# Loading granule 5's keys and queries ahead of granule 4's values, and releasing the loads of granules 6 and 7 at another point

## The chip, the cores and the metric

The kernel runs on one core of a Trainium2 chip. The metric is device microseconds of one execution; lower is better. Engines are named as in the profile: PE is TensorE's matmuls, PEld its weight loads, DVE is VectorE, ACT is ScalarE, POOL is GpSimd, SP is SyncE.

## The reference

Attention of 4 batches x 8 heads x 768 rows x 64, with a mask (8 global keys, 96 local ones) and a linear bias, followed by a two-layer feed-forward block with a squared ReLU:

```python
scores = scale * np.matmul(q, k.transpose(0, 1, 3, 2))
scores = np.where(keep, scores + bias, -1000000000.0)
a = softmax(scores)                     # (cut)
x = np.matmul(a, v)                     # -> (3072, 512)
h = x @ w_in                            # 512 -> 2048
out = (s * np.maximum(h, 0)**2 + b) @ w_out
```

## The kernel before

The 3072 rows are cut into 12 granules of 256 (numbered 0 to 11, three in each batch; all numbers here count from 0). For each granule GpSimd loads keys, queries and values (128 KB each piece, cast from f32 to bf16), the keys and queries are transposed (by TensorE for granules 0 to 3, by DMA transposes from SyncE from granule 4 on), then TensorE makes scores and weighted sums, and the sums, transposed once more (tile xT, below "transposed sums"), go into the feed-forward block. Work of several granules is interleaved by hand so that TensorE always has something to do.

```python
    def load_granule(j):                      # k and q of both blocks, then v
        ...
        load_v(j)

    def hold_loads(ap):                       # a 1x1 copy on GpSimd: later loads wait for `ap`
        g = work.tile([P, 1], BF16, name="gate", tag="gate")
        nc.gpsimd.tensor_copy(g[0:1, :], ap)
    # (cut)
    def qk_by_dma(j):                         # four DMA transposes of one granule
        for i in range(GB):
            for n in range(2):
                nc.sync.dma_start_transpose(qk_of(b, n)[:, g * GB + i], nat[j][:, n, i, :, :]...)
    # (cut)
    def finish_granule(j):
        if j < X_PE:
            x_by_pe(j)                        # transposed sums by TensorE
        else:
            x_by_dma(j)                       # transposed sums by DMA
        if 6 <= j + LEAD < NJ:                # LEAD = 4
            hold_loads(xT[j][0:1, 0, GT - 1 : GT])
            load_granule(j + LEAD)
    # (cut: the order in which granules 3 to 5 are loaded)
    for i in range(GB):
        load_qk(4, i)
    load_v(3)
    load_v(4)
    load_granule(5)
```

The softmax here doesn't subtract the row's maximum and nothing guards it: scores larger than these inputs give would overflow.

Of the kernel before, what the change touches and what calls it, by code (L numbers as in the profile page):

```python
# [17 lines left out]
def kernel(  # L18
# [19 lines left out]
    DM = H * D  # L38
    DF = moe_w_in.shape[1]
    GB = 2  # L40
# [5 lines left out]
    NJ = B * NGR  # L46
# [22 lines left out]
    LEAD = 4  # L69
# [12 lines left out]
    def nat_tile(j):  # L82
        if j not in nat:
            nat[j] = ldp.tile([P, 2, GB, H, D], BF16, name="nat", tag=f"nat{j % 4}", bufs=1)
        return nat[j]
# [3 lines left out]
    def rows_of(src, b, sb):  # L89
        return src[b, :, sb * P : (sb + 1) * P, :].rearrange("h p d -> p h d")  # L90
# [8 lines left out]
    def load_qk(j, i):  # L99
        b, g = divmod(j, NGR)  # L100
        for n in range(2):
            nc.gpsimd.dma_start(nat_tile(j)[:, n, i, :, :], rows_of(srcs[n], b, g * GB + i))  # L102

    def load_v(j, blocks=range(GB)):
        b, g = divmod(j, NGR)
        for i in blocks:
            sb = g * GB + i
            nc.gpsimd.dma_start(vbuf[b % 2][:, sb, :, 0:D], rows_of(v, b, sb))  # L108

    def load_granule(j):  # L110
        b, g = divmod(j, NGR)
        t = nat_tile(j)
        for i in range(GB):
            sb = g * GB + i
            for n in range(2):
                nc.gpsimd.dma_start(t[:, n, i, :, :], rows_of(srcs[n], b, sb))  # L116
        load_v(j)


    def hold_loads(ap):  # L120
        g = work.tile([P, 1], BF16, name="gate", tag="gate")
        nc.gpsimd.tensor_copy(g[0:1, :], ap)  # L122
# [119 lines left out]
    def template(hs):  # L242
        for h in hs:
            nc.scalar.activation(tmpl[:, h, 0:3, :], late_bf[:, 0:3, :], ACT.Exp, scale=slopes[h])
# [25 lines left out]
    xn = {}  # L270
# [312 lines left out]
    def x_by_pe(j, evac=(nc.vector.tensor_copy, nc.scalar.copy)):  # L583
        t = xT_tile(j)
        nk = KC // len(evac)
        for e, ev in enumerate(evac):
            ps = ps_h.tile([P, nk, GT], BF16, name="ps_x", tag="psh")
            for kc in range(nk):
                for i in range(GB):
                    c = (e * nk + kc) * P  # L590
                    nc.tensor.transpose(
                        ps[:, kc, i * P : (i + 1) * P], xn[j][:, i, c : c + P], ident_bf[:]
                    )
            ev(t[:, e * nk : (e + 1) * nk, :], ps[:])  # L594

    def x_by_dma(j):
        t = xT_tile(j)
        for i in range(GB):
            nc.sync.dma_start_transpose(t[:, :, i * P : (i + 1) * P], xn[j][:, i, :])
# [350 lines left out]
    def finish_granule(j):  # L950
        if j < X_PE:
            x_by_pe(j)
        else:
            x_by_dma(j)
        if 6 <= j + LEAD < NJ:
            hold_loads(xT[j][0:1, 0, GT - 1 : GT])
            load_granule(j + LEAD)

    def step(s, c0, c1, c2, pool=None, pre=()):
# [22 lines left out]
        if last:  # L982
            finish_granule(j)
            if SHIFT < j + 2 < NJ:
                load_voff(j + 2)
# [92 lines left out]
    for i in range(GB):  # L1078
        load_qk(4, i)
    load_v(3)  # L1080
    load_v(4)
    load_granule(5)
    template(range(H))
    lo = FC - FC // 4
    p2_mm(0, 0, 0, lo)
# [34 lines left out]
    p2_mm(1, 1, FC // 2 + 3, FC)  # L1120
    p2_hold(1, 1)
    finish_granule(2)
    s6 = scores(6)
    run(s6)
# [12 lines left out]
    make_koff(4)  # L1137
    run(p1[2][6:8])
    finish_granule(3)
    run(scores(8))  # L1140
    make_voff(4)
# [110 lines left out]
```

## Time and profile before

| | before |
|---|---|
| median of 3 runs | 208.91 us (208.49 to 209.06) |
| the profiled run | 209.15 us, span 207.4 us |
| TensorE busy, weight loads busy | 97%, 77% |
| TensorE's one wait for a transfer | 0.51 us, at 69.1 us |

How to read it: in the slices each digit is a fortieth of the span in tenths of busy time. A line of a timeline gives the start, the length, the engine, the source line, the operation and its tiles; idle time and what ended it stand in brackets. The prediction shows the lines.

### The profile page before, as it was taken

The numbers are of one execution on the slowest core, as the hardware profiler recorded it, in microseconds if no ns is written. First come the engines' busy times: TensorE is split into PE (matmuls) and PEld (weight loads), VectorE is DVE, ScalarE is ACT, GpSimd is POOL, SyncE is SP. The second block draws the span as 40 slices with busy tenths as digits, with TensorE's granted clock in tenths as the row PEclk, the third lists the DMA queues.
The fourth block names the chain that finished last, engine by engine and source line by source line (L and its number), as shares of the span: only waits on it lengthen the run. The fifth ranks groups of instructions, "written<-read, shape, count | busy, mean of one in ns | idle before, by whom it ended". The sixth has DMA issues, their size and how long they took to land.

```text
span 207.4 us, 5323 instructions
## 1 busy us (share of the span) xinstructions
PE 202.1 (97%) x2191; PEld 160.1 (77%) x2191; DVE 161.3 (78%) x338; ACT 128.5 (62%) x198; POOL 68.9 (33%) x90
## 2 busy tenths in 40 slices
PE   7999999999999999999999999999999999999993
PEld 2678884557867485878888898888888889888883
DVE  7786599977989856799799974699866696737974
ACT  5875669486976548786664595663695764476200
POOL 8985333799365300810900828200000000000000
PEclk9999999999999999999999999999999999999999
DMA  5999999999999999999999999999570300240006
GB/s 164 172 179 202 207 206 177 155 152 129 110 150 120 151 132 218 155 213 212 152 198 153 125 154 178 194 172 126 52 206 0 95 14 0 56 150 0 0 9 196
DMA packets 110836, 28.17 MB, mean 136 GB/s; under 512 B 97852, under 2 KB 109308, under 8 KB 110812
## 3 DMA queue, kind: packets, MB, share of 16 engines
q0 software_dynamic: 76000, 13.11, 90.1%
q1 hardware_dynamic: 33612, 14.13, 41.7%
q10 hardware_dynamic: 1200, 0.59, 1.1%
q8 instruction: 17, 0.28, 0.6%
q14 instruction: 7, 0.06, 0.1%
HBM read 27.26 MB, written 6.29 MB: 162 GB/s over the span
## 4 chain that ended last, share of the span: by engine, by line
PE 65%; DMA 23%; POOL 9%; issue 1%; DVE 0%; POOLq 0%
PE ps L619 29%; PE ps L819 24%; DMA nat<-in_q_dram 12%; DMA w_in_bf<-in_moe_w_in_dram 6%; PE ps L667 5%; DMA qx<-nat 4%; PE ps_s L441 4%; PE ps_av L495 3%; POOL vb L108 3%; POOL nat L102 3%; POOL w_in_bf L140 2%; POOL nat L116 1%; PE ps_last L819 0%; DVE o_last L828 0%; POOL rel L173 0%
## 5 line engine op out<-in xcount | busy, mean ns | idle before, releaser
L619 PE MATMUL ps<-xT,w_in_bf 128*128 128x256 bf16 x768 | 90.3, 273 | 0.0
L629 ACT ACTIVATE gT<-ps 128x512 bf16<-128x512 f32 x96 | 55.8, 599 | 46.8 <-PE ps L619 46.6
L619 PEld LDWEIGHTS <-w_in_bf 128*128 128x128 bf16 x768 | 73.0, 98 | 9.4 <-DVE xT L594 0.2
L450 ACT ACTIVATE pt<-ps_s 128x1024 bf16<-128x1024 f32 (+1 forms) x44 | 39.3, 946 | 3.3 <-PE ps_s L441 3.3
L667 PE MATMUL ps<-w_out_bf,gT 128*128 128x512 bf16 x128 | 29.7, 380 | 0.0
L457 DVE TENSOR_TENSOR pt<-pt,tmpl 128x1024 bf16<-128x1024 bf16 (+1 forms) x40 | 24.6, 645 | 3.8 <-ACT pt L450 3.7
L819 PEld LDWEIGHTS <-gsum 128*128 128x128 bf16 x256 | 24.1, 98 | 3.7 <-DVE gsum L782 0.5
L108 POOL DMA_DIRECT2D vb<-in_v_dram x24 | 21.4, 906 | 6.9 <-DMA w_out_bf<-in_moe_w_out_dram 3.4
L793 DVE TENSOR_TENSOR gT<-gT 128x1024 bf16<-128x1024 bf16 x20 | 13.7, 686 | 11.7 <-ACT gT L629 11.7
L667 PEld LDWEIGHTS <-gT 128*128 128x128 bf16 x128 | 11.7, 98 | 13.0
L466 DVE TENSOR_TENSOR xn<-ps_av,rc 128x256 bf16<-128x256 f32 x48 | 20.4, 425 | 1.7
L819 PEld LDWEIGHTS <-gT 128*128 128x128 bf16 x200 | 18.6, 98 | 2.3
L465 DVE RECIPROCAL rc<-ps_av 128x4 f32<-128x4 f32 x48 | 8.6, 179 | 12.3 <-PE ps_av L495 10.4
L116 POOL DMA_DIRECT2D nat<-in_k_dram x16 | 14.2, 885 | 9.2 <-DMA nat<-in_k_dram 5.1
L495 PEld LDWEIGHTS <-pt 128*128 128x128 bf16 x320 | 14.4, 97 | 2.7 <-DVE xn L466 0.7
L632 DVE TENSOR_TENSOR gT<-gT 128x512 bf16<-128x512 bf16 x32 | 13.0, 422 | 3.5 <-ACT gT L629 3.3
L495 PE MATMUL ps_av<-vb,pt 128*128 128x65 bf16 x208 | 15.5, 193 | 0.0
L819 PE MATMUL ps<-w_out_bf,gsum 128*128 128x256 bf16 x128 | 15.3, 273 | 0.0
L116 POOL DMA_DIRECT2D nat<-in_q_dram x16 | 14.2, 888 | 2.9 <-DMA w_in_bf<-in_moe_w_in_dram 1.9
L819 PE MATMUL ps<-wsub,gsum 128*128 128x256 bf16 x128 | 15.1, 273 | 0.0
L819 PE MATMUL ps<-w_out_bf,gT 128*128 128x256 bf16 x120 | 13.9, 273 | 0.0
L122 POOL COPY gate<-xT 1x1 bf16<-1x1 bf16 x6 | 1.1, 176 | 35.9 <-DMA xT<-xn 35.9
(112 smaller groups left out, 228.5 us busy)
## 6 DMA issues: line engine op xcount, KB each, us to landing
out_dram<-o_q SPq DMA_DIRECT2D x15, 256.0 KB, 2.6
vb<-in_v_dram POOLq DMA_DIRECT2D x24, 128.0 KB, 8.3
nat<-in_k_dram POOLq DMA_DIRECT2D x22, 128.0 KB, 7.7
nat<-in_q_dram POOLq DMA_DIRECT2D x22, 128.0 KB, 7.6
w_out_bf<-in_moe_w_out_dram POOLq DMA_DIRECT2D x4, 512.0 KB, 16.2
w_in_bf<-in_moe_w_in_dram POOLq DMA_DIRECT2D x4, 256.0 KB, 7.4
w_in_bf<-in_moe_w_in_dram POOLq DMA_DIRECT2D x2, 512.0 KB, 11.3
out_dram<-o_sb SPq DMA_DIRECT2D x4, 256.0 KB, 6.3
```

What stands on the lines that cost most here:

```text
L108: nc.gpsimd.dma_start(vbuf[b % 2][:, sb, :, 0:D], rows_of(v, b, sb))
L116: nc.gpsimd.dma_start(t[:, n, i, :, :], rows_of(srcs[n], b, sb))
L450: nc.scalar.activation(pt[:, :, 0:ncol], ps[:, :, 0:ncol], ACT.Exp, scale=QSCALE)
L457: nc.vector.tensor_tensor(pv, pv, m.rearrange("p h a c -> p h (a c)"), ALU.mult)
L466: nc.vector.tensor_tensor(dst, av[:, :, :, 0:D], rc[:].to_broadcast((P, 2, 2, D)), ALU.mult)
L495: nc.tensor.matmul(av[:, i, hi, 0 : D + 1], lhsT=pt[:, hi, c * P : (c + 1) * P], rhs=vv, start=(n == 0), stop=(n == len(terms) - 1),)
L619: nc.tensor.matmul(ps[:, i, :], lhsT=w_in_bf[:, kc, fc * P : (fc + 1) * P], rhs=xT[j][:, kc, :], start=(kc == 0), stop=(kc == KC - 1),)
L629: nc.scalar.activation(gs, ps[:], ACT.Relu)
L632: nc.vector.tensor_tensor(gs, gs, gs, ALU.mult)
L667: nc.tensor.matmul(po[:], lhsT=g_of(j)[:, fc, tb * P : (tb + 1) * P], rhs=w_out_bf[:, fc, :], start=(fc == 0), stop=(fc == FC - 1),)
L793: outs.append(lambda: nc.vector.tensor_tensor(gs, gs, gs, ALU.mult))
L819: nc.tensor.matmul(ps[:, tb, cs], lhsT=stat[:, fc, tb * P : (tb + 1) * P], rhs=mov[:, fc, cs], start=(fc == 0), stop=(fc == NH - 1),)
```

## The change

Intent: let granule 5's keys and queries land earlier by loading them ahead of granule 4's values, and keep the loads of granules 6 and 7 out of the way of granule 5's transposes by releasing them only at granule 3's last weighted sum. Before, granule 6 was released by granule 2's transposed sums and granule 7 by granule 3's.

```diff
-        if 6 <= j + LEAD < NJ:
+        if j == 3:
+            hold_loads(xn[j][0:1, GB - 1, DM - 1 : DM])
+            load_granule(6)
+            load_granule(7)
+        elif 8 <= j + LEAD < NJ:
             hold_loads(xT[j][0:1, 0, GT - 1 : GT])
             load_granule(j + LEAD)
 (cut)
     load_v(3)
+    for i in range(GB):
+        load_qk(5, i)
     load_v(4)
-    load_granule(5)
+    load_v(5)
```

## The prediction

> **What bounds the kernel now.** I read the page first (busy shares and slices), then the waits of TensorE alone, then the chain that ended last, and then the timelines of TensorE, GpSimd and VectorE around the one wait that mattered. The page:
>
> ```profile
> span 207.4 us, 5323 instructions
> PE 202.1 (97%) x2191; PEld 160.1 (77%) x2191; DVE 161.3 (78%) x338; ACT 128.5 (62%) x198; POOL 68.9 (33%) x90
> PE   7999999999999999999999999999999999999993
> DMA  5999999999999999999999999999570300240006
> ```
>
> TensorE is busy in 38 of 40 slices at nine tenths or more; only the first and last are lower, which are the opening and the tail. All its idle time is 207.4 - 202.1 = 5.3 us. The DMA engines are full for three quarters of the span, so transfers can be late, but that costs time only where TensorE waits. The waits of TensorE's matmuls, complete:
>
> ```profile
> PE ps_w L161 <- DVE idle L151: 1.2, 1, 1.2
> PE ps_s L441 <- DMA qx<-nat: 0.5, 1, 0.5
> ```
>
> The first is the warm-up at the start. The second is the only wait for a transfer in the whole kernel. The chain of waits from 38 to 70 us says where it comes from:
>
> ```profile
> 48.56 11.61 DMA nat<-in_q_dram
> 60.17 0.02 issue
> 60.19 8.86 DMA qx<-nat
> 69.06 0.04 issue
> 69.10 0.57 PE ps_s L441 x14
> ```
>
> A load of queries (granule 5's second block, by its place in the issue order) was issued at 48.56, landed at 60.17, was turned by a DMA transpose from 60.19 to 69.06, and TensorE's scores for granule 5 began again at 69.10. Behind this point the chain is TensorE without a break to 204.1 us, then the last eviction. The timeline of TensorE at that wait, and the same 16 score matmuls eight microseconds later for comparison:
>
> ```profile
> 68.36 0.23 PE L441 MATMUL ps_s<-qx,kx 64*128 64x128 bf16 x2
> 69.10 0.34 PE L441 MATMUL ps_s<-qx,kx 64*128 64x128 bf16 x6 [0.51 <-DMA qx<-nat]
> 69.60 3.63 PE L667 MATMUL ps<-w_out_bf,gT 128*128 128x512 bf16 x16
> ...
> 77.13 0.40 PE L441 MATMUL ps_s<-qx,kx 64*128 64x128 bf16 x8
> 77.37 0.39 PE L441 MATMUL ps_s<-qx,ko 64*128 64x128 bf16 x8
> 77.69 3.63 PE L667 MATMUL ps<-w_out_bf,gT 128*128 128x512 bf16 x16
> ```
>
> Undisturbed, the 16 take 77.69 - 77.13 = 0.56 us until the next group starts; with the wait they take 69.60 - 68.36 = 1.24 us. So the stall delays TensorE's starts by 0.68 us (0.51 is what is left after the modelled tail of the second matmul).
>
> **What the Trainium skill says.** "Perfetto Trace Analysis", section "Identifying the Most-Contended Engine", warns that matmul busy share is no measure of the distance to roofline, and names the weight-load share instead. Here that is 77%, so 97% does not mean peak; but a change in load order removes no matmul, so it can only win idle time, and the section "Optimization Strategy" of that page says to look for the gaps of that engine and the semaphore behind them. The trace has one such gap. "DMA: Bandwidth & Descriptors", section "Issuing engines are not separate DMA queues", says that transfers started by different engines run on the same 16 DMA engines and interleave. The trace agrees: while loads were in flight the transpose of 60.19 took 8.86 us from issue to landing, and one issued at 80.08, in a stretch without new loads, 4.9 us (from the view of the tile qx). The same page, "Queues, rings and completion order", says that on each DMA engine the descriptors of one ring are consumed in ring order, though completion is not strictly first in, first out; the loads of GpSimd from 27 us on landed in issue order, which is what I rest the landing times below on.
>
> **The change part by part.** The built instruction order shows that TensorE, VectorE, ScalarE and SyncE have the same instructions in the same order; only buffer numbers differ. GpSimd has 93 rows instead of 94: one 1x1 gate copy (0.18 us, off the path) falls away. Everything else is the order and release of loads on GpSimd, whose timeline before is:
>
> ```profile
> 49.43 1.77 POOL L108 DMA_DIRECT2D vb<-in_v_dram  x2
> 51.16 0.18 POOL L122 COPY gate<-xT 1x1 bf16<-1x1 bf16 x1
> 51.28 0.88 POOL L116 DMA_DIRECT2D nat<-in_k_dram  x1
> ...
> 56.19 0.88 POOL L116 DMA_DIRECT2D nat<-in_k_dram  x1 [3.05 <-DMA nat<-in_k_dram]
> ...
> 61.62 0.18 POOL L122 COPY gate<-xT 1x1 bf16<-1x1 bf16 x1
> ```
>
> Neither gate made GpSimd wait: no idle time stands beside them. What holds it back is the landing of the load eight before (3.05 us at 56.19).
>
> Part one, the order. Numbering granules from 0: before, the eight issues from 44.08 on are two of v4 (landed 50.09 and 51.98), four of k and q of granule 5 (55.91, 57.31, 57.97, 60.17) and two of v5 (60.57, 61.77). All are 128 KB of the same shape, so I keep the eight landing slots and put the new order into them: k5 and q5 at about 50.1, 52.0, 55.9, 57.3; v4 at about 58.0 and 60.2; v5 as before. The last query block thus lands 60.17 - 57.3 = 2.9 us earlier. SyncE issued its four transposes of granule 5 at 55.92, 57.32, 58.61 and 60.19; it is free after 53.57, so they can go at about 53.6, 55, 56.2 and 57.5. With the old 8.86 us the last lands at 66.4; with the 4.9 us of the quiet stretch, at 62.4. TensorE asks at 68.40. Either way the stall of 0.68 us goes.
>
> Part two, the release. Granule 6's first two loads were issued at 51.28 and 52.27 and flew beside granule 5's transposes until 65.2 and 66.4. Now they wait for the last weighted sum of granule 3, which VectorE writes here:
>
> ```profile
> 57.66 0.42 DVE L466 TENSOR_TENSOR xn<-ps_av,rc 128x256 bf16<-128x256 f32 x1
> ...
> 62.31 0.54 DVE L396 COPY vo<-vb 128x1056 bf16<-128x1056 bf16 x1
> ```
>
> So they start at about 58.1 + 0.2 for the gate = 58.3, seven microseconds later, and the four k and q issues of 0.88 us stand back to back to 61.8. That takes the competitor from the transposes of granule 5 (an argument for less than 8.86 us). The queue does not run dry: v4 and v5 are still in flight to about 61. With the 5.0 us from issue to landing of the quiet issue at 83.87 as a floor and 1.2 us per piece, my estimate is landings at 64, 65, 66.5 and 67.5; before they were 65.2, 66.4, 69.4 and 69.8. Granule 6 is not later, because before it was the queue and not the gate that held it. Granule 7 follows at about 63.5 instead of 61.7, with the last of its keys and queries at 79.5 before.
>
> Sum: 0.68 us of stall removed on the path; 0.18 us of GpSimd off it; nothing added to any compute engine. Taking 0.6 to 0.65 as what arrives at the end gives 208.91 - 0.63 = 208.28, say 208.3.
>
> **The rivals.** First, the wait moves to v4. It lands up to 8 us later, and VectorE copies it at 62.31 (the second line of the last fence), TensorE uses it at 65.16. Slack: 62.31 - 60.2 = 2.1 us. If contention adds over 2 us, VectorE, which works in order, stalls, and TensorE would feel only what exceeds the next 2.8 us; the time would be 208.9 to 209.5. Unlikely. Second, the wait moves to granule 6. Its scores start at 81.73; its last transpose was issued at 70.70 and, with some 7 us, landed at about 77.7. That is 4 us of slack, so the late release would have to cost over 4 us beyond my estimate; then 208.9 to 210. The full DMA queue speaks for it a little, the landing estimate against. Third, the 0.68 us are given back later: granule 5's transposed sums landed at 97.59 and TensorE used them at 98.35, a slack of 0.7 us. This transfer starts after VectorE's work on granule 5, which itself moves up with TensorE, so most of the gain should pass. If it does not, 208.9 stays. Fourth, a larger gain: nothing in the waits of TensorE offers more than the 0.68 us, for the weight-load waits after 69 us for VectorE or DMA sum to 1.4 us in seven pieces that the change does not touch.
>
> **Range and chances.** The three runs of before spread from 208.49 to 209.06, which is as large as the effect. I take 207.7 to 208.9: the gain lost altogether at the upper end; at the lower end the whole gain, on top of a run population half a microsecond quicker. Two per cent is 4.2 us; the stall cannot give that, and a loss of that size needs a new stall six times the old one. Faster 0.01, within 2% 0.98, slower 0.01.
>
> **What would show it.** Right: no wait of TensorE for qx at scores of granule 5; the last transpose of granule 5 issued near 57.5 and landed before 66.5; v4 landing at 58 to 60 with no idle time of VectorE before its copy; the gate copy at about 58.3 with idle time before it; granule 6's keys and queries landed by 70; the group after the scores of granule 5 starting near 68.9. Wrong: a wait of TensorE on ps_s or on voff in the stretch 60 to 95 us, a transpose still over 9 us, or granule 6's transposes landing after 81.

## The result

| | before | after |
|---|---|---|
| median of 4 runs, same rounds | 208.72 us (208.49 to 209.06) | 208.82 us (208.71 to 209.06) |
| the profiled run | 209.15 us | 209.06 us |

The ratio is 1.0005, with a 95% interval of 0.9986 to 1.0024: the same. A ratio here is the mean time of one kernel's fast runs over that of the other's of the same rounds, so it is not quite the ratio of the medians.

The measured time lies in the predicted range, but the predicted gain of 0.63 us did not come. The page of the changed kernel, then the waits of TensorE's matmuls, complete:

```profile
span 207.3 us, 5312 instructions
PE 201.9 (97%) x2183; PEld 160.2 (77%) x2191; DVE 160.6 (77%) x338; ACT 128.4 (62%) x198; POOL 70.3 (34%) x89
```

```profile
PE ps_w L161 <- DVE idle L151: 1.2, 1, 1.2
PE ps_s L441 <- ACT qx L331: 0.3, 1, 0.3
PE ps L667 <- issue: 0.2, 1, 0.2
```

The wait for the transposed queries is gone, as meant. (Eight records of L667 matmuls are missing in this trace, which is what the last line sees; the weight loads have no gap there.) A wait of 0.3 us for line 331 stands near the start; the second profile of the unchanged kernel (before_2, below) has it too, so it is not the change's. TensorE's timeline at granule 5's scores:

```profile
68.89 0.40 PE L441 MATMUL ps_s<-qx,kx 64*128 64x128 bf16 x8
69.12 0.39 PE L441 MATMUL ps_s<-qx,ko 64*128 64x128 bf16 x8
69.44 2.76 PE L667 MATMUL ps<-w_out_bf,gT 128*128 128x512 bf16 x11
```

The 16 score matmuls run through in 0.55 us. But they begin at 68.89 and not at 68.36: TensorE came here 0.53 us later than in the profile of before. The delay did not arise where the change is. It is there from the first 8 us on, in which both programs are the same. The timeline of TensorE in the opening, before:

```profile
5.29 0.72 PE L327 MATMUL ps_t<-ident_bf,nat 128*128 128x128 bf16 x8
5.85 0.81 PE L416 MATMUL ps_s<-open_bf 128*128 128x384 bf16 x4
6.68 0.51 PE L441 MATMUL ps_s<-qx,kx 64*128 64x128 bf16 x12
```

and after:

```profile
5.30 1.11 PE L327 MATMUL ps_t<-ident_bf,nat 128*128 128x128 bf16 x8
6.20 1.31 PE L416 MATMUL ps_s<-open_bf 128*128 128x384 bf16 x4
7.45 0.51 PE L441 MATMUL ps_s<-qx,kx 64*128 64x128 bf16 x12
```

The same four matmuls of 384 columns start 0.16 us apart in the one and 0.32 us apart in the other: TensorE still ran at half clock. The trace's clock record has the rise to full clock at 5.14 us before and at 7.20 us after. At 6.7 us the two are 0.77 us apart, at 12 us 0.61, at 68 us 0.53.

The Trainium skill has this in "TensorE: Matmul & The Clock Gate", section "What's actually happening": the clock gate follows a free-running activity window of about 3.4 us, so the moment of full clock varies from run to run. The traces agree: over the 14 profiles the rise lies between 3.92 and 7.23 us, and rise and fall of the clock are 201.39 or 204.80 us apart, two values that differ by 3.41 us.

GpSimd's timeline shows that the release now does hold the loads:

```profile
58.79 0.31 POOL L122 COPY gate<-xn 1x1 bf16<-1x1 bf16 x1 [7.75 <-DVE xn L466]
59.28 0.88 POOL L116 DMA_DIRECT2D nat<-in_k_dram  x1 [0.18 <-issue]
```

### The profile page after: what moved, and what is told of

Same layout as the page of the kernel before. It is cut to its first block, busy times and chain, and to the rows that moved or that the text cites. A ratio compares the mean times of both kernels' runs of the same rounds, so it can differ in the third digit from the quotient of the medians.

```text
span 207.3 us, 5312 instructions
## 1 busy us (share of the span) xinstructions
PE 201.9 (97%) x2183; PEld 160.2 (77%) x2191; DVE 160.6 (77%) x338; ACT 128.4 (62%) x198; POOL 70.3 (34%) x89
## 4 chain that ended last, share of the span: by engine, by line
PE 95%; DMA 2%; DVE 0%; issue 0%; ACT 0%
PE ps L619 41%; PE ps L819 24%; PE ps L667 13%; PE ps_s L441 6%; PE ps_av L495 5%; DMA first<-in_k_dram 2%; PE ps_t L351 1%; PE ps_s L517 1%; PE ps_t L327 1%; PE ps_x L591 1%; PE ps_s L416 1%; PE ps_s L532 1%; PE ps_av L558 1%; PE ps_t L341 0%; PE ps_last L819 0%
## 5 line engine op out<-in xcount | busy, mean ns | idle before, releaser
L667 PE MATMUL ps<-w_out_bf,gT 128*128 128x512 bf16 x120 | 28.7, 380 | 0.5 <-issue 0.2
L108 POOL DMA_DIRECT2D vb<-in_v_dram x24 | 21.9, 924 | 3.3 <-DMA w_out_bf<-in_moe_w_out_dram 2.9
L667 PEld LDWEIGHTS <-gT 128*128 128x128 bf16 x128 | 11.8, 98 | 13.0
L116 POOL DMA_DIRECT2D nat<-in_k_dram x14 | 12.4, 888 | 3.9 <-DMA w_in_bf<-in_moe_w_in_dram 2.3
L116 POOL DMA_DIRECT2D nat<-in_q_dram x14 | 12.7, 909 | 2.1 <-DMA w_in_bf<-in_moe_w_in_dram 2.1
```

The lines of the kernel that those rows point to most:

```text
L108: nc.gpsimd.dma_start(vbuf[b % 2][:, sb, :, 0:D], rows_of(v, b, sb))
L116: nc.gpsimd.dma_start(t[:, n, i, :, :], rows_of(srcs[n], b, sb))
L667: nc.tensor.matmul(po[:], lhsT=g_of(j)[:, fc, tb * P : (tb + 1) * P], rhs=w_out_bf[:, fc, :], start=(fc == 0), stop=(fc == FC - 1),)
```

## The experiments

**Theory A (absorption).** In the kernel before, TensorE goes on with granule 5's scores at the later of two times: its own arrival, which moves with the moment of full clock, and the landing of the last transposed queries, which does not. A late clock is taken up by that wait; there is then nothing for the change to remove. With an early clock the change removes the wait, and the next landing may take the time back. **Theory B (given back later).** The stall is always there, the change always removes it, and the stretch behind it becomes longer.

Twelve runs of nine kernels were made with 5 rounds each. For each profile I read the arrival at granule 5's scores (start of the first one), the start of the group behind them, and the start of the last product. One expression turned out to hold in 13 of the 14, the first pair included: time of the profiled run = start of the group behind the scores + 139.5 to 139.6 us. In after_2 it is 139.9. The stretch from that group to the last product is 133.60 to 133.69 us in the 13, and 134.02 in after_2.

(All in us; the last product is a group of 16 matmuls of line 819.)

| profile | full clock at | arrival | last query transpose landed | next group starts | last product starts | profiled run |
|---|---|---|---|---|---|---|
| before | 5.14 | 68.36 | 69.06 | 69.60 | 203.22 | 209.15 |
| before_2 | 7.23 | 68.89 | 68.40 | 69.44 | 203.04 | 208.94 |
| before_3 | 4.12 | 68.60 | 68.58 | 69.15 | 202.76 | 208.67 |
| after | 7.20 | 68.89 | 65.55 | 69.44 | 203.13 | 209.06 |
| after_2 | 5.51 | 68.30 | 66.11 | 68.96 | 202.98 | 208.89 |
| after_3 | 4.13 | 68.30 | 65.58 | 68.85 | 202.54 | 208.44 |
| order_only | 6.68 | 68.58 | 66.73 | 69.14 | 202.74 | 208.63 |
| order_only_2 | 5.04 | 68.25 | 67.14 | 68.80 | 202.42 | 208.33 |
| release_only | 6.48 | 68.52 | 66.96 | 69.08 | 202.74 | 208.66 |
| order_ko | 4.98 | 68.26 | 66.38 | 68.81 | 202.44 | 208.34 |
| v7_late | 4.25 | 68.55 | 66.95 | 69.22 | 202.89 | 208.79 |
| late5 | 6.13 | 68.51 | 70.50 | 71.04 | 204.64 | 210.53 |
| late5_pad | 6.55 | 69.60 | 70.79 | 71.33 | 204.93 | 210.83 |
| after_pad | 3.92 | 69.26 | 65.43 | 69.86 | 203.53 | 209.42 |

### before_2 and before_3: the kernel before, unchanged

No edit.

> The kernel before, unchanged, for more runs and a second profile. Theory A (absorption): TensorE's clock came to full at 5.14 us in the first profile of before and at 7.20 us in that of after, in a stretch where both programs are the same; this puts TensorE 0.76 us behind, and in the kernel before such a delay is taken up by the wait for granule 5's queries. So ratio to before 1.000; in this profile the sum of opening delay (against the first profile of before) and of the stall at granule 5's scores is near 0.7 us, whatever its parts. Theory B (the gain is given back later): the stall is 0.6 to 0.7 us again, whatever the opening, and the stretch after 69 us is what differs from after.

> The kernel before once more, for a third profile. Theory A: the start of granule 5's scores after the wait is the later of TensorE's arrival (68.3 with an early clock, 68.9 with a late one) and the landing at 68.4 to 69.1; the last matmul starts near 203.6 to 203.8 in either case. Ratio 1.000.

Measured: before_2 208.59 us median (208.43 to 208.94), ratio 1.000 (0.9988 to 1.0013); before_3 208.40 us (208.21 to 208.87), ratio 0.9991 (0.9976 to 1.0006). The timeline of before_2 at granule 5's scores:

```profile
68.89 0.40 PE L441 MATMUL ps_s<-qx,kx 64*128 64x128 bf16 x8
69.13 0.39 PE L441 MATMUL ps_s<-qx,ko 64*128 64x128 bf16 x8
69.44 2.76 PE L667 MATMUL ps<-w_out_bf,gT 128*128 128x512 bf16 x11
```

This is the kernel before, and it has no wait here: its lines are those of after, to 0.01 us. The clock came late (7.23 us), TensorE arrived at 68.89, and the queries had landed at 68.40. So the stall of 0.68 us, on which the prediction rests, is not a property of the kernel; it is what remains when an early clock meets a late landing. That part of Theory A is shown, and Theory B falls where it says that the stall is always there. The expectation that opening delay and stall sum to 0.7 us held roughly for before_2 (0.53 + 0 at this point). It failed for before_3: an early clock, yet an arrival at 68.60, because small waits before 60 us had cost 0.3 us, and a landing at 68.58, so no stall. Its last matmul started at 203.44 (203.89 in before, 203.72 in before_2), outside the expected 203.6 to 203.8. The time of before is thus not constant; the wait only cuts off its lower part. An early clock helps only to a point, too: at 12 us, TensorE is equally far to 0.11 us in the eight profiles with the rise at 3.92 to 5.51 us.

### after_2 and after_3: the changed kernel, unchanged

No edit.

> The changed kernel, unchanged. Theory A: no stall at granule 5's scores; its time follows the moment at which the clock came to full, about 208.2 when that is before 5.3 us, up to 209 when it is after 7; mean over the runs 0.2 to 0.4 us below before (ratio 0.998 to 0.999). Theory B: the same time as before whatever the opening, ratio 1.000 to 1.001, and a longer stretch from granule 5's scores to the end than in before.

> The changed kernel once more, for a third profile and more runs beside those of order_only_2. Theory A (absorption, with a row of landings): no wait for granule 5's queries; if the clock comes before 5.6 us, 0.2 to 0.6 us are lost to the shift copies of granule 5's keys and to granule 4's sums; if it comes after 6.4, nothing is lost. Mean 208.6 to 208.8, ratio 1.000. If the first prediction's sum were right after all, ratio 0.997.

Measured: after_2 208.76 us (208.22 to 209.13), ratio 1.0008 (0.9994 to 1.0021); after_3 208.47 us (208.41 to 209.07), ratio 0.9996 (0.9981 to 1.0011). In after_2 the clock came early and TensorE arrived at 68.30 with the queries there, which is the case that the prediction counted on. Its timeline goes on:

```profile
68.30 0.40 PE L441 MATMUL ps_s<-qx,kx 64*128 64x128 bf16 x8
68.63 0.40 PE L441 MATMUL ps_s<-qx,ko 64*128 64x128 bf16 x8
68.96 3.41 PE L667 MATMUL ps<-w_out_bf,gT 128*128 128x512 bf16 x14
...
83.63 1.91 PE L619 MATMUL ps<-xT,w_in_bf 128*128 128x256 bf16 x16 [0.40 <-DMA xT<-xn]
```

Two things take the time back. The second half of the scores starts 0.33 us after the first instead of 0.23, since it reads the shift copies of granule 5's keys (tile ko: in the code, the keys of the blocks from one before). VectorE made them late; its timeline:

```profile
67.09 0.83 DVE L383 COPY ko<-kx 128x1024 bf16<-128x1024 bf16 x1
67.96 0.62 DVE L384 COPY ko<-kx 128x64 bf16<-128x64 bf16 x1
```

In after_3 the first of these copies took 0.42 us, in order_only_2 the second took 0.18. GpSimd was issuing loads from 66.82 to 67.69 and from 67.69 to 68.57, and both copies end within 0.25 us of these ends. "SBUF — State Buffer", section "Who interferes with whom" of the Trainium skill says that GpSimd shares a port pair with some VectorE copies, and whoever comes second is blocked for the whole instruction; these lines fit, but no run here isolates it. The larger loss is the 0.40 us at 83.63: granule 4's transposed sums landed only at 83.49, while TensorE would have asked at about 83.2.

In after_3, with the clock at 4.13 us, the copies ended at 68.05 and the sums landed at 82.67; nothing was lost, and that run took 208.44 us. My expectation of 0.2 to 0.6 us lost with an early clock missed there. So the taking back happens in some early runs and not in others. The expected gain in the mean (ratio 0.998 to 0.999) missed too: after_2 had 1.0008, and what Theory B had said of this run, a ratio of 1.000 to 1.001 and a longer stretch behind the scores, is what came. Neither theory alone describes the changed kernel.

### order_only, release_only and order_only_2: one part alone

order_only takes the second hunk of the change, release_only the first; order_only_2 repeats order_only.

```diff
# order_only, order_only_2
     load_v(3)
+    for i in range(GB):
+        load_qk(5, i)
     load_v(4)
-    load_granule(5)
+    load_v(5)
# release_only
-        if 6 <= j + LEAD < NJ:
+        if j == 3:
+            hold_loads(xn[j][0:1, GB - 1, DM - 1 : DM])
+            load_granule(6)
+            load_granule(7)
+        elif 8 <= j + LEAD < NJ:
```

> Granule 5's keys and queries ahead of granule 4's values, but granules 6 and 7 released as before. Theory A: the last query block lands near 57, its transpose near 66; no stall, or under 0.1 us; the same time as after within 0.2 us. Rival (the release does the work): the transposes still fly beside granule 6's first loads and land at 68 to 69, so a stall of 0.2 us or more stays.

> Granules 6 and 7 released by granule 3's last weighted sum, order of the loads as before. Theory A: the last query block lands near 60.2 as before, its transpose issued at 60.2 lands at 67 to 68.5, since two loads fewer are beside it; the stall is 0 to 0.2 us. Rival (the order does the work): landing at 69 again and a stall like that of before.

> The order alone, again; it had the lowest mean so far (208.46 in 5 runs, against 208.75 in 10 of after). If the release costs something: mean again 0.2 us or more below that of after_3, ratio to before 0.999. If the 208.46 was the luck of early clocks: the same as before, ratio 1.000.

Measured: order_only 208.38 us (208.31 to 208.68), ratio 0.9997 (0.9985 to 1.0009); release_only 208.66 us (208.25 to 208.68), ratio 1.000 (0.9988 to 1.0012); order_only_2 208.63 us (208.33 to 208.82), ratio 0.9998 (0.9984 to 1.0012). Either part alone brings the last transpose to 66.7 to 67.1, from 68.4 to 69.1, and no stall is left: the order by an earlier issue (57.68 against 59.79 to 60.23), the release by a shorter flight (59.82 to 66.96 is 7.14 us, against 8.17 to 8.86 in the three profiles of before). Both rivals named there fall, and the parts do not add up, since one suffices. The suspicion that the release costs something was not borne out: order_only_2 has a mean of 208.62 in 6 runs, after_3 of the same rounds 208.57. The traces do show a small cost that the means cannot: between 99 and 100.5 us TensorE loses 0.06 to 0.07 us in all six profiles with the release and in none of the eight without. Its cause is not known.

### late5, late5_pad and after_pad: the wait made large, and useless work put before it

```diff
# late5, against before
     load_v(3)
     load_v(4)
-    load_granule(5)
+    load_v(5)
+    for i in range(GB):
+        load_qk(5, i)
# late5_pad, against late5; after_pad, against after
+    warm(5, 4 * P)        # five matmuls of 512 columns, 1.08 us, that nothing reads
     template(range(H))
```

> The kernel before with granule 5's keys and queries behind all values (v3, v4, v5, then k and q of 5). The last query block takes the slot of the last v5, about 1.5 us later, so its transpose lands near 70 instead of 68.4 to 69.1. Theory A (TensorE goes on at the later of its own arrival, 68.3 to 68.9, and this landing): scores go on near 70; a stall of 1.1 to 1.7 us; time 209.6 to 210.2, ratio about 1.005, and less spread than before since no opening is late enough to show. Theory B (given back later): ratio under 1.002.

> The kernel of late5 with five more warm-up matmuls of 512 columns on TensorE at about 31 us, 5 x 0.216 = 1.08 us of work that nothing needs. Theory A: TensorE arrives at 69.4 to 70.0 instead of 68.3 to 68.9, the transpose still lands near 70, so the time is that of late5 within 0.2 us: over a microsecond of TensorE work costs nothing. Theory B: late5 plus 1.08 us, ratio to before higher by 0.005.

> The changed kernel with the same five useless matmuls. Theory A: no landing is left to take them up at granule 5's scores, and the one at granule 4's transposed sums moves with the work, so the time is after's plus 0.9 to 1.1 us, near 209.8, ratio 1.005 to 1.006. Theory B: the same. The pair with late5_pad tells them apart, not this run alone.

Measured: late5 211.52 us median of 6 (210.04 to 212.67), ratio 1.0133 (1.0097 to 1.017); late5_pad 210.92 us (210.67 to 211.07), ratio 1.0108 (1.0095 to 1.0121); after_pad 209.68 us (209.42 to 209.76), ratio 1.0047 (1.0035 to 1.0059). The timeline of late5:

```profile
68.51 0.23 PE L441 MATMUL ps_s<-qx,kx 64*128 64x128 bf16 x2
70.54 0.34 PE L441 MATMUL ps_s<-qx,kx 64*128 64x128 bf16 x6 [1.80 <-DMA qx<-nat]
```

and of late5_pad:

```profile
69.60 0.23 PE L441 MATMUL ps_s<-qx,kx 64*128 64x128 bf16 x2
70.83 0.34 PE L441 MATMUL ps_s<-qx,kx 64*128 64x128 bf16 x6 [1.00 <-DMA qx<-nat]
```

TensorE arrives 1.09 us later and goes on only 0.29 us later, which is the difference of the two landings (70.50 and 70.79). In the run times, late5_pad's mean of 210.90 is 0.44 us above the 210.46 of the three late5 runs that kept their clock (see below): more than the expected 0.2, but well under the 1.08 of Theory B. In after_pad, with no such wait, the same work costs nearly all of itself: its mean of 209.63 is 0.94 us above the 208.68 of all runs of after, and its last product starts 1.11 us behind that of order_only_2, the profile with the earliest end. So a landing does take up TensorE's lateness here, and the landing sets the time 1:1 once it is the later of the two. That is the core of Theory A, shown at a size well above the noise.

Late5's times miss the expected 209.6 to 210.2 and the expected small spread. The landing was 0.5 us later than I had put it (70.5 for 70), because SyncE was not free for the last transpose before 62.03. And three of its six runs took 212.2 to 212.7 us with a mean granted clock of 0.992, the other three 210.0 to 210.8 with 0.997 to 1.000. A deficit of 0.008 of 210 us is 1.7 us of clock; at half clock that is 3.4 us of time, as long as the window named above. The longer idle of 1.8 us may have let the clock fall once. But this mean counts every stretch at half clock, also one at the end (in late5's profile the clock fell at 207.51 of 208.8 us, mean 0.997), and no profile caught such a run, so this stays argued. Late5_pad, whose idle was shorter, had no such run among four.

### v7_late and order_ko: attempts at a version without landings in its way

```diff
# v7_late, against after
             load_granule(6)
-            load_granule(7)
+            for i in range(GB):
+                load_qk(7, i)
         elif 8 <= j + LEAD < NJ:
             hold_loads(xT[j][0:1, 0, GT - 1 : GT])
+            if j == 4:
+                load_v(7)
             load_granule(j + LEAD)
# order_ko, against order_only: the shift copies before the weighted sum
         run(c0)
+        if not last and j + 1 == QK_PE + 1:
+            make_koff(j + 1)
         stage_A(2 * s)
         flush()
-        if not last and j + 1 == QK_PE + 1:
-            make_koff(j + 1)
```

> The changed kernel, with granule 7's two value loads moved behind the gate on granule 4's transposed sums. In the second profile of after, whose clock came early (5.51 us), TensorE waited 0.40 us for these sums, which landed at 83.49 beside granule 7's values (80.61 and 83.31). Theory A: they land by 82.5, that wait goes in every opening, and the time follows the opening alone: 208.1 with an early clock, 208.8 with a late one; mean ratio 0.998 to 0.999, which would be the best of all. Rival (the transpose is not slowed by these two loads): sums still land after 83 and the time is that of after.

> The order alone, and VectorE's two shift copies of granule 5's keys put ahead of the first weighted sum of granule 4's step, about 1.2 us earlier, so that they end before 67. Theory A: TensorE never waits for them, and this is the version with the fewest landings in its way: end follows the clock, 208.1 with an early one, 208.7 with a late one; mean ratio 0.998 to 0.9995. Rival: the copies delay VectorE's sums and so TensorE's next weighted sums; ratio 1.001.

Measured: v7_late 208.67 us (208.54 to 208.91), ratio 1.0002 (0.9989 to 1.0015). Its sums landed at 81.05 and that wait was gone, as expected, but the mean did not fall: with the clock at 4.25 us, TensorE lost 0.37 us (against order_only_2) to granule 4's queries, which had landed at 59.38 (58.3 to 59.1 elsewhere), and 0.1 us to the shift copies. Order_ko 208.41 us (208.32 to 208.68), ratio 0.9991 (0.9976 to 1.0006): the copies moved to 65.30 and no wait for a transfer is left; the run with the clock at 4.98 us took 208.34 us. That is the lowest mean of all versions, 208.45 us in 6 runs, but its interval includes 1, and the unchanged before_3 had a mean of 208.47 in the same rounds, so a version that beats both is not shown.

## Why the prediction was right or wrong

Pooling the sessions, 48 runs of before have a mean of 208.63 us (standard deviation 0.25) and 16 of after one of 208.68 us (0.28). The difference is 0.06 +- 0.16 us; the predicted -0.63 us is excluded. That the time still fell in the range is luck as far as the mechanism goes.

**The stall of 0.68 us.** This is the step that failed: "Sum: 0.68 us of stall removed on the path". It took one profile's stall for a constant. Measured in three profiles of before it is 0.68, 0 and 0 us, because the arrival moves from 68.36 to 68.89 with the clock and the landing from 68.40 to 69.06. Where the stall was absent the change had nothing to win: before_2 and after both start the next group at 69.44, not near 68.9 as the prediction's list of signs has it. The profile that I was given was the one with the full stall. By the sum above, a landing at 69.06 makes a run of about 69.06 + 0.54 + 139.5 = 209.1 us (an estimate), and only 2 of the 48 runs of before took that long. The landings of before_2 and before_3 give 208.4 and 208.6, inside what the arrivals alone give (68.30 to 68.89: 208.4 to 208.9). How much of the missing gain is a stall that was not there, and how much was taken back behind it, the runs without a profile do not show.

**The new landing times.** That loads land in issue order was read from the traces and held; the passage cited beside it is on the queues of SyncE and ScalarE, and these loads are GpSimd's. The times held to within 0.7 us for granule 5's first two pieces, its last and v4: k and q landed at 49.94, 51.30, 53.34 and 56.85 (predicted 50.1, 52.0, 55.9, 57.3), v4 at 57.43 and 59.69 (58.0, 60.2). The third piece came 2.6 us earlier than its slot, which had been late in the first profile (in before_2 it was filled at 53.30; of the others only v7_late has it late again, 55.77). The last v5 came 2.8 us later than said (64.52), without effect. The last transpose was issued at 57.99 (57.5) and landed at 65.55 (62.4 to 66.4).

**The release.** The gate copy came at 58.79 with 7.75 us of idle time before it (58.3; VectorE was late with the rest of the opening). Granule 6's keys and queries landed at 66.33 to 69.48: later than the estimate of 64 to 67.5, but before 70. "Granule 6 is not later" did not quite hold: the first two landed 0.8 to 1.1 us later than in the profile of before and the last 0.4 us earlier, and against before_2 (63.73 to 68.79) all four were later. No wait came of it.

**The rivals.** The first two did not happen: no wait on v4 or on granule 6 appears in any profile of the changed kernel. The third, that the gain is given back later, is the one that came true in part, and by a transfer one granule earlier than I had named. I computed a slack of 0.7 us for granule 5's transposed sums and did not look at granule 4's, which landed at 83.24 in the profile of before with TensorE's matmuls starting at 83.91. In after_2 they took 0.40 us back. (In the fourth, the 1.4 us of weight-load waits are six pieces, not seven.)

**The range.** It held because it allowed for the gain being lost, not because the sum was right.

## What to carry to other kernels

Before counting a stall on the path as a gain, ask what sets both sides of it: if the waiting engine's arrival varies from run to run and the landing does not, the stall is what is left over in the lucky runs, and one profile cannot tell its mean. When the slack of the landings behind it is as small as the stall, list all of them with landing and use, not the one that comes to mind. An experiment that makes the wait large and then adds useless work before it shows in two runs whether it absorbs.

## What the Trainium skill lacked or had wrong

- "TensorE: Matmul & The Clock Gate", section "What you observe", gives the warm-up as around 4 us +-500 ns. Here, with warm-up matmuls from 1.19 us on, the rise came 2.7 to 6.0 us after them (3.92 to 7.23 us in 14 profiles). The same page's free-running window fits this (the range is 3.31 us), the +-500 ns does not. What it cost at 12 us was 0 to 0.6 us, as much as this change could win.
- No page says that a transfer that TensorE waits for later absorbs such an opening delay: 1.09 us of added TensorE work cost 0.29 us in late5_pad, of which all was a later landing.
- "DMA: Bandwidth & Descriptors" has no time for a small DMA transpose beside a full queue of loads. Of the same transposes of keys and queries, those issued between 46 and 70 us, beside the loads, took 6.6 to 10.1 us from issue to landing in the 14 profiles (10.1: granule 4's last in v7_late), and the one issued near 80 us, in a stretch without new loads, 2.4 to 5.8 us.
